# Divisor rows by fp32 matmul, a start by head, 16-row bit copies and a new filler rule in a fused attention and gated-convolution kernel

## The chip, the cores and the metric

The kernel runs on one core of one Trainium2 chip. The time is the device time of one execution in microseconds (us). Engines are named as in the profile: PE is TensorE's matmuls, PEld its weight loads, DVE is VectorE, ACT is ScalarE, POOL is GpSimd, SP is SyncE (it issues nearly all DMA transfers here, 269 of the 274 that the profile of before lists).

## The reference

Four batches, eight heads, 768 positions, head size 64. Attention is masked by hash buckets: each position gets six sign bits from a projection, and only keys with the same six bits count.

```python
q_bits = (einsum('bhsd,dk->bhsk', q, proj) > 0);  k_bits = ...
mask   = q_bucket[:, :, :, None] == k_bucket[:, :, None, :]
scores = where(mask, scale * (q @ k^T), -1e9)
attn   = exp(scores - max);  attn /= attn.sum(-1) + 1e-9
x      = (attn @ v) as (batch, 768, 512)
```

The result goes through a gated long convolution:

```python
x1, x2, x3 = split(x @ w_proj)                     # 3 x 512 columns
x2_conv    = irfft(rfft(x2) * rfft(filter_fft))    # along the 768 positions
out        = (x1 * x2_conv * x3) @ w_out
```

## The kernel before

The kernel works on "pairs": two heads of one batch, 16 pairs in all, four for each batch. For a pair, q and k are split into fp16 high and low parts (`hl`), transposed by DMA into `pr_q` and `pr_k` (channels on partitions), and the sign bits are written below the channels as extra rows of the contraction. A match adds a known constant to the score, so one biased exp does the masking.

The planner uses them for fillers: matmuls of a constant tile `warm`, whose result nobody reads, put into gaps that the planner expects on TensorE, meant to keep its clock up (its mean is 0.965 to 0.970 with 52 of them in e3 and 0.977 to 0.992 with 194 in e1, both below). This is the rule of before:

```python
WARM_COLS, WARM_UNTIL, WARM_FILL = 256, 115000.0, 0.7
if book.warm is not None and s < WARM_UNTIL and gap > 350.0 and before:
    room = w0 + WARM_FILL * gap         # 0.7 of a gap over 350 ns, until 115 us
    ...                                 # fillers of 256 columns while they fit
```

The bits are compared in one go into a tile `bt`, and four copies of 12 rows take them to their places:

```python
for i in range(4):
    nc.load(row[("q", "k")[i // 2]][HD : HD + NBIT, i % 2, :],
            bt[32 * i : 32 * i + NBIT, :], SMALL)      # NBIT = 12, SMALL = SyncE
```

After attention times v (`pv`, copied to `S` and summed to `T`), the row sums are turned by DMA (`lt`), inverted (`rl`), and spread over the 64 partitions of each head through a row in DRAM:

```python
nc.load(lt[:, par, :], S[r0 : r0 + 1, 0:SEQ], SMALL)                    # hop 1
...                                                                     # rl = 1 / lt
nc.load(rdr.rearrange("h (p c) -> p h c", p=P), rl, SMALL)              # hop 2, to DRAM
nc.load(R[HD*par : HD*par+HD, :], rdr[par:par+1, :].to_broadcast([HD, SEQ]), SMALL)  # hop 3
nc.vector.scalar_tensor_tensor(U, in0=T[:, 0:SEQ], scalar=vsd, op0=ALU.add, in1=R, op1=ALU.mult)
```

`U` is split again (`xh`, `xl`), and with the four pairs of a batch the projection can begin: its first matmuls are called `x2a`, its last ones `wout`. All instructions are recorded first; a planner with a cost for each then sets the order on each engine and writes it out. Every change of the program or of a cost therefore gives a new order of everything.

The softmax here doesn't subtract the row's maximum and nothing guards it: scores larger than these inputs give would overflow.

## Time and profile before

| | before |
|---|---|
| time, median | 463.37 us (the first three runs, 461.76 to 463.63; the result below has a fourth) |
| profiled span | 461.0 us |
| first score matmul | 14.7 us |
| first x2a (batch 0's projection) | 111.9 us |
| first wout | 190.8 us |
| span minus first wout | 270.2 us |

A chain here is the work followed back from the last instruction: at each step to what released it. The page of the kernel before, cut to the span, TensorE's busy tenths in 40 slices, its granted clock in tenths and the chain of work that ended last:

```profile
span 461.0 us, 7071 instructions
PE   7688987969899999999999999999999999999996
PEclk9789999879999999999999999999999999999999
...
PE 71%; DMA 12%; DVE 9%; ACT 3%; issue 3%; SPq 1%; DVEq 0%; ACTq 0%; POOLq 0%
PE x L232 24%; PE pv L232 10%; PE stp L232 9%; PE wout L232 9%; PE x2b L232 6%; PE x2a L232 6%; DMA pr_q<-hl 4%; PE zps L232 2%; DMA lt<-S 2%; ACT pt L232 2%; DMA w<-in_moe_w_proj_dram 2%; PE fdft L232 2%; DMA pr_k<-hl 1%; DMA R<-rdr 1%; DMA rdr<-rl 1%
```

The first ten slices (115 us) have holes and a clock that drops, to 7 or 8 tenths in four of them; later TensorE is full. The view by windows says the same; its columns are the stretch, its length, then the busy time of PE, PEld, DVE, ACT and POOL with instruction counts, the granted clock, the DMA share and GB/s:

```profile
80.00:100.00 20.00, 15.20 (x75) 6.43 (x75) 14.30 (x26) 8.62 (x13) 5.46 (x7) 0.80 0.89 195
180.00:200.00 20.00, 20.00 (x113) 10.85 (x112) 12.26 (x25) 12.39 (x17) 2.62 (x3) 1.00 0.77 183
200.00:460.00 260.00, 255.66 (x1519) 139.16 (x1517) 162.74 (x301) 125.47 (x182) 48.69 (x41) 1.00 0.25 65
```

From 180 us on TensorE is busy for 20.00 of 20 and 255.66 of 260 us, so there is little to win except by removing TensorE work. Before that, what TensorE waits for decides.

The next view is the timeline of TensorE in a stretch of before (start, length, engine, operation, count, and in brackets the idle time before and what ended it); `warm` marks fillers:

```profile
48.18 0.49 PE L232 MATMUL stp<-pr_q,pr_k 76*128 76x512 f16 x2
48.51 0.49 PE L229 MATMUL stp<-warm 128*128 128x256 f16 x3
49.06 0.48 PE L232 MATMUL stp<-pr_q,pr_k 76*128 76x512 f16 x2
49.39 0.49 PE L229 MATMUL stp<-warm 128*128 128x256 f16 x3
50.05 0.48 PE L232 MATMUL stp<-pr_q,pr_k 76*128 76x512 f16 x2 [0.17 <-ACT pt L232]
```

And ScalarE at the same time:

```profile
48.12 5.33 ACT L232 ACTIVATE pt<-stp,nmatch 128x768 f16<-128x768 f32 x6
```

Each pair of score matmuls is followed at once by its fillers, the fillers end before the exp of their tile begins, and ScalarE does six exps in 5.33 us, 0.89 us each, without a gap. Two score tiles are enough to keep it fed.

### The profile page before, as it was taken

The numbers are of one execution on the slowest core, as the hardware profiler recorded it, in microseconds if no ns is written. First come the engines' busy times: TensorE is split into PE (matmuls) and PEld (weight loads), VectorE is DVE, ScalarE is ACT, GpSimd is POOL, SyncE is SP. The second block draws the span as 40 slices with busy tenths as digits, with TensorE's granted clock in tenths as the row PEclk, the third lists the DMA queues.
The fourth block names the chain that finished last, engine by engine and source line by source line (L and its number), as shares of the span: only waits on it lengthen the run. The fifth ranks groups of instructions, "written<-read, shape, count | busy, mean of one in ns | idle before, by whom it ended". The sixth has DMA issues, their size and how long they took to land.

```text
span 461.0 us, 7071 instructions
## 1 busy us (share of the span) xinstructions
PE 431.6 (94%) x2590; PEld 233.4 (51%) x2590; DVE 305.9 (66%) x552; ACT 252.8 (55%) x348; POOL 112.2 (24%) x117
## 2 busy tenths in 40 slices
PE   7688987969899999999999999999999999999996
PEld 5244544425355456544455665544556664445652
DVE  4667687949593899734588879225677873279870
ACT  5679979358146752777565766665666632200102
POOL 4103297223031521212232211113242010122000
PEclk9789999879999999999999999999999999999999
DMA  9988679798845324765372323451010103100003
GB/s 273 201 213 207 159 213 251 165 202 216 201 110 148 86 58 76 183 162 155 79 135 71 75 71 74 141 131 48 3 40 2 34 4 107 66 0 1 0 2 137
DMA packets 101187, 51.88 MB, mean 113 GB/s; under 512 B 83520, under 2 KB 92816, under 8 KB 101152
## 3 DMA queue, kind: packets, MB, share of 16 engines
q1 hardware_dynamic: 99472, 51.00, 43.3%
q10 hardware_dynamic: 1552, 0.39, 0.4%
q8 instruction: 20, 0.33, 0.3%
q14 instruction: 15, 0.12, 0.1%
q0 software_dynamic: 128, 0.04, 0.0%
HBM read 32.02 MB, written 6.39 MB: 83 GB/s over the span
## 4 chain that ended last, share of the span: by engine, by line
PE 71%; DMA 12%; DVE 9%; ACT 3%; issue 3%; SPq 1%; DVEq 0%; ACTq 0%; POOLq 0%
PE x L232 24%; PE pv L232 10%; PE stp L232 9%; PE wout L232 9%; PE x2b L232 6%; PE x2a L232 6%; DMA pr_q<-hl 4%; PE zps L232 2%; DMA lt<-S 2%; ACT pt L232 2%; DMA w<-in_moe_w_proj_dram 2%; PE fdft L232 2%; DMA pr_k<-hl 1%; DMA R<-rdr 1%; DMA rdr<-rl 1%
## 5 line engine op out<-in xcount | busy, mean ns | idle before, releaser
L232 ACT ACTIVATE pt<-stp,nmatch 128x768 f16<-128x768 f32 x192 | 168.6, 899 | 65.1 <-PE stp L232 62.4
L232 PE MATMUL stp<-pr_q,pr_k 76*128 76x512 f16 (+1 forms) x384 | 96.3, 334 | 11.2 <-ACT pt L232 8.5
L232 PE MATMUL x<-xh,wph 128*128 128x384 f16 x256 | 83.4, 326 | 0.5 <-DVE bt L232 0.2
L232 PE MATMUL x<-xl,wph 128*128 128x384 f16 x256 | 83.4, 326 | 0.0
L232 PE MATMUL x<-xh,wpl 128*128 128x384 f16 x256 | 83.4, 326 | 0.0
L232 PE MATMUL pv<-pt,vt 128*128 128x257 f16 (+1 forms) x384 | 76.4, 333 | 1.4 <-DVE bt L232 1.4
L232 PEld LDWEIGHTS <-wph 128*128 128x128 f16 x512 | 49.7, 97 | 34.6 <-issue 2.2
L232 DVE SCALAR_TENSOR_TENSOR T<-S,cst_sb,pv 64x512 f32<-64x512 f32 x64 | 38.3, 608 | 36.8 <-ACT S L232 35.9
L232 PEld LDWEIGHTS <-pr_k 76*128 76x128 f16 x384 | 36.9, 99 | 49.8 <-issue 22.8
L232 POOL TENSOR_TENSOR xl<-R,xh 128x768 f16<-128x768 f32 x16 | 26.3, 1641 | 133.1 <-DVE xh L232 112.4
L232 PEld LDWEIGHTS <-vt 128*128 128x128 f16 x384 | 37.8, 99 | 29.8 <-issue 5.9
L232 ACT COPY S<-pv 64x512 f32<-64x512 f32 (+1 forms) x48 | 22.8, 476 | 43.1 <-PE pv L232 39.1
L232 PEld LDWEIGHTS <-wpl 128*128 128x128 f16 x256 | 25.0, 97 | 16.1
L232 POOL TENSOR_TENSOR vt<-nat_v,vt 128x768 f16<-128x768 f32 x16 | 26.2, 1641 | 17.9 <-ACT vt L232 17.0
L232 PEld LDWEIGHTS <-xh 128*128 128x128 f16 x192 | 18.7, 97 | 20.7 <-issue 0.3
L232 DVE TENSOR_SCALAR bt<-zps,cst_sb 128x384 f16<-128x384 f32 x30 | 17.5, 610 | 16.2 <-PE zps L232 15.7
L232 ACT ACTIVATE osb<-wout 128x512 f32<-128x512 f32 x24 | 14.3, 596 | 24.7 <-PE wout L232 24.6
L232 POOL CAST vt<-nat_v 128x768 f16<-128x768 f32 x11 | 9.0, 823 | 74.1 <-PE pv L232 74.1
L232 DVE SCALAR_TENSOR_TENSOR R<-T,vsd,R 128x768 f32<-128x768 f32 x16 | 16.2, 1012 | 14.6 <-DMA R<-rdr 14.6
L232 DVE SCALAR_TENSOR_TENSOR hl<-nat_k,hl 128x768 f16<-128x768 f32 x16 | 16.3, 1016 | 12.2 <-ACT hl L232 12.1
L232 DVE TENSOR_TENSOR fu<-x2b,x2s 128x512 f32<-128x512 f32 x12 | 8.3, 688 | 23.6 <-PE x2b L232 23.6
L232 ACT ACTIVATE hl<-nat_k 128x768 f16<-128x768 f32 x16 | 13.5, 844 | 14.7 <-DMA pr_k<-hl 9.1
(339 smaller groups left out, 673.5 us busy)
## 6 DMA issues: line engine op xcount, KB each, us to landing
nat_k<-in_k_dram SPq DMA_DIRECT2D x16, 384.0 KB
nat_v<-in_v_dram SPq DMA_DIRECT2D x16, 384.0 KB
R<-rdr SPq DMA_DIRECT2D x32, 192.0 KB
out_dram<-osb SPq DMA_DIRECT2D x24, 256.0 KB
nat_q<-in_q_dram SPq DMA_DIRECT2D x15, 384.0 KB
w<-in_moe_w_proj_dram SPq DMA_DIRECT2D x12, 256.0 KB
w<-in_moe_filter_fft_dram SPq DMA_DIRECT2D x6, 256.0 KB
w<-in_moe_w_out_dram SPq DMA_DIRECT2D x4, 256.0 KB
```

Source lines behind the costliest of these rows:

```text
L232: o["done"] = getattr(getattr(nc, o["lane"]), o["method"])(*[sub(x) for x in o["args"]], **{n: sub(x) for n, x in o["kw"].items()})
```

## The change

Its intent was to start earlier and to shorten the way from `T` to `U`, and so to bring the first x2a forward. It has six parts: (1) for pairs 0 to 3 and 15, the rows of `rl` are spread by an fp32 matmul with a selector `sel` instead of the DRAM row; (2) the first pair is prepared head by head, and the loads behind it are held until its data are in work; (3) bit rows in copies of 16 instead of 12; (4) the queues of the bit copies and of the weight loads get constants of their own, which name SyncE, as before, so this part changes nothing; (5) new costs in the planner, among them a model of shared DMA time; (6) a new rule for fillers.

The core of the diff, with cuts marked (the remark behind `R_PE` is this document's):

```diff
+ROWS = 16
...
-            if book.warm is not None and s < WARM_UNTIL and gap > 350.0 and before:
+            if book.warm is not None and gap > 40.0 and before:
                 w0 = free[e]
-                room = w0 + WARM_FILL * gap
-                while True:
-                    ... # pieces of 256 columns
+                while w0 < s:
+                    cold = active.get(int(w0 // 3413) - 1, 0.0) < 1640.0
+                    if not cold and gap < WARM_GAP:
+                        break
+                    room = free[e] + WARM_FILL[0 if cold else 1] * gap - w0
+                    c = [n for n in WARM_COLS if n / (1.2 if cold else 2.4) <= room]
...
-WARM_COLS, WARM_UNTIL, WARM_FILL = 256, 115000.0, 0.7
+WARM_COLS, WARM_GAP, WARM_FILL = (256, 128, 64), 350.0, (1.0, 0.9)
...
-                row[("q", "k")[i // 2]][HD : HD + NBIT, i % 2, :], bt[32 * i : 32 * i + NBIT, :], SMALL
+                row[("q", "k")[i // 2]][HD : HD + ROWS, i % 2, :], bt[32 * i : 32 * i + ROWS, :], BITQ
...
+        if g in R_PE:                      # R_PE = (0, 1, 2, 3, 15)
+            row = U[0:2, :]
+            for par in range(2):
+                nc.load(row[par : par + 1, :], rl[:, par, :], SMALL)
+            for hf in range(2):
+                rp = psW.tile([P, HALF], FP32, tag="w", name="rp")
+                nc.tensor.matmul(rp, sel, row[:, cs])
+                nc.vector.scalar_tensor_tensor(U[:, cs], in0=T[:, cs], scalar=vsd,
+                    op0=ALU.add, in1=rp, op1=ALU.mult)
+        else:
+            ...                            # the DRAM row, as before
...
-        load_qk(0, "p", "s")
-        hilo(0)
-        turn_pe(0)
-        zbits(0, True)
+        for par in range(2):
+            first_loads(par)
+        first_turn(0)
+        load_qk(1, None, None, True)
+        first_turn(1)
...                                        # new planner costs, cut
```

## The prediction

> **What bounds the kernel now.** The windows view splits the 461.0 us span in two. From 180 us on TensorE is nearly always busy. Before that the chain of waits runs through "DMA pr_q<-hl", "lt<-S", "rdr<-rl", ACT and DVE. Counting TensorE's order at its warm pace (512 columns 0.216 us, 384 columns 0.162, sixteen zps 0.76) gives about 391 us of work, 57 us of it ahead of the first x2a, which starts at 111.95 us. So about 41 us are lost there (half-clock stretches, waits, 126 fillers of 13 us) and about 15 us later. Only the first loss is worth attacking.
>
> Why: (a) The first score matmul starts at 14.74 us, after `ident` (5.5 us on the GpSimd queue), two-head transposes and bits. (b) SyncE is nearly full: from 28 to 112 us its issues last 74 of 84 us (timeline): transposes 1.4 to 2.4 us, 12-row bit copies 0.8 us each, four per pair, the 128-row `lt` 0.55. (c) From the end of T to U take 18, 23, 26 and 26 us for pairs 0 to 3: three DMA hops, one through DRAM, then DVE's order. Pair 3's U (108.95 us) gates x2a.
>
> **What the change does.**
> - Pairs 0 to 3 and 15: the DRAM row and two 192 KB broadcasts become two row copies and two fp32 matmuls: one hop and 0.39 MB less per pair. [...]
> - 16-row bit copies: [...]I expect 0.55 us, 1 us of SyncE per pair.
> - First pair by head: first scores at about 11 us; zps of pair 1 at 19 us, from 22.7.
> - New planner costs: the built order moves x2a from after 144 score matmuls to after 132; fillers 126 to 224, now also beyond 115 us, where a planned gap stands around ida (about 3 us of fillers).
>
> **Sum.** Up to pair 3's U, SyncE's issues would end near 70 us, ACT (60 exps of 0.9 us, hl, vt) near 77, DMA (share 0.8 to 0.9, less broadcasts) near 80. Waits among them add some 10: first x2a at about 91 us. After it stand 340 us of TensorE work (4.7 us done ahead before now come later, and one rp pair) and about 17 us of loss: span 448; the timed runs lie 2.4 us above the traced span.
>
> Predicted 450 us (3% faster), 440 to 459 eight times in ten; faster by over 2% 0.70, within 2% 0.26, slower 0.04.
>
> **What would show it.** First score near 11 us; `pr<-bt` issues near 0.55 us; T to U under 15 us for pairs 0 to 3; first x2a at 86 to 96 us; ACT busier from 20 to 90 us; rp about 0.65 us; after x2a the same saturation.
>
> **What would make it wrong.** DMA engines, not SyncE, may hold the transposes (the share reaches 1.14 at 90 to 100 us): x2a then stays beyond 100 us. The gap around ida may exceed its fillers, or weights come late. DVE's order may hold U though the row is ready. If the new order fits the chip better than I allow, x2a comes before 85 us.

## More of the kernel before

Runs of one kernel still differ by 1 to 7 us, so a single trace shows a mechanism well and a difference of 2 us badly.

One score tile is 128 keys by 768 queries. It lies in a PSUM tile of 1024 fp32 columns, of which there are two:

```python
stp = psS.tile([P, 1024], FP32, tag="s", name="stp")        # two buffers
for lo_c, hi_c in ((0, 512), (512, SEQ)): ...               # SEQ is 768; two matmuls, cut
    nc.tensor.matmul(stp[:, lo_c:hi_c], kp[kr, ts(jt, P)], qp[kr, lo_c:hi_c])
nc.scalar.activation(pt[:, 0:SEQ], stp[:, 0:SEQ], AF.Exp, bias=nmatch, scale=LSCALE)
```

The last 256 columns of the tile hold no scores.

## The result

| | before | after |
|---|---|---|
| time, median | 462.56 us (four runs, 461.74 to 463.63) | 478.46 us (four runs, 477.80 to 480.20) |
| ratio, 95% interval | | 1.0348, 1.0309 to 1.0387: slower |
| profiled span | 461.0 us | 476.0 us |
| first score matmul | 14.7 us | 11.0 us |
| first x2a | 111.9 us | 119.2 us |
| first wout | 190.8 us | 204.0 us |
| span minus first wout | 270.2 us | 272.0 us |

Ratios, here and below, are ratios of fast runs, with a 95% interval; they are not quite the ratio of the medians that are quoted.

The change makes the kernel 3.5% slower. Of the 15.0 us that the span is longer, 13.2 us are there at the first wout; what comes after takes the same time within 2 us. The page of the kernel after, the lines that answer to those of before:

```profile
span 476.0 us, 7319 instructions
PE   8797969969999999999999999999999999999996
PEclk9797897989999999999999999999999999999999
...
PE 79%; DVE 14%; ACT 4%; issue 2%; DVEq 0%; ACTq 0%
PE x L245 22%; PE pv L245 12%; PE stp L245 12%; PE wout L245 9%; PE x2a L245 7%; PE x2b L245 7%; PE stp L198 4%; ACT pt L245 4%; PE zps L245 2%; DVE hl L245 2%; DVE cv L245 2%; PE fdft L245 1%; DVE uv L245 1%; PE rp L245 1%; PE idrq L245 1%
```

Fillers (`stp L198`) and exps (`ACT pt`) are now in the chain that ended last, with 4% each; in before the fillers were not in it and the exps had 2%. The waits through DMA that the change aimed at (`DMA lt<-S`, `rdr<-rl`, `R<-rdr`) are no longer among the fifteen largest; DMA, with 12% of the chain before, is not in it at all, and VectorE has 14% in place of 9%. So something of what was intended happened, and another thing came beside it. TensorE's windows of after, to be read against those of before:

```profile
80.00:100.00 20.00, 16.70 (x99) 8.86 (x99) 13.96 (x18) 13.39 (x18) 13.81 (x12) 0.91 0.74 163
180.00:200.00 20.00, 19.37 (x134) 11.47 (x133) 19.62 (x43) 6.75 (x11) 1.65 (x1) 1.00 0.68 159
200.00:460.00 260.00, 259.09 (x1537) 141.04 (x1536) 163.88 (x321) 129.66 (x187) 32.51 (x29) 1.00 0.24 63
```

TensorE is busier from 80 to 100 us than before (16.70 against 15.20 us) and yet later with its work: the fillers in this stretch take 3.14 us, in before 0.93 us. Where the time goes is seen in the timeline of TensorE in a stretch of after with the same work as the one shown of before:

```profile
37.56 0.24 PE L198 MATMUL stp<-warm 128*128 128x128 f16 x2 [0.99 <-ACT pt L245]
37.65 0.49 PE L245 MATMUL stp<-pr_q,pr_k 80*128 80x512 f16 x2
37.98 0.49 PE L198 MATMUL stp<-warm 128*128 128x256 f16 x3
39.52 0.32 PE L198 MATMUL stp<-warm 128*128 128x128 f16 x2 [1.05 <-ACT pt L245]
39.65 0.83 PE L245 MATMUL stp<-pr_q,pr_k 80*128 80x512 f16 x2
40.27 0.85 PE L198 MATMUL stp<-warm 128*128 128x256 f16 x3
42.16 0.32 PE L198 MATMUL stp<-warm 128*128 128x128 f16 x2 [1.05 <-ACT pt L245]
42.30 0.83 PE L245 MATMUL stp<-pr_q,pr_k 80*128 80x512 f16 x2
```

and of ScalarE:

```profile
36.61 0.90 ACT L245 ACTIVATE pt<-stp,nmatch 128x768 f16<-128x768 f32 x1 [0.17 <-PE stp L198]
38.56 0.90 ACT L245 ACTIVATE pt<-stp,nmatch 128x768 f16<-128x768 f32 x1 [1.05 <-PE stp L198]
41.21 0.90 ACT L245 ACTIVATE pt<-stp,nmatch 128x768 f16<-128x768 f32 x1 [1.75 <-PE stp L198]
```

Read them as one story. At 36.61 us an exp begins. TensorE's next instruction is a filler of 128 columns into the same tile as that exp reads. It waits until the exp is over (idle 0.99 us, ended by ScalarE) and starts at 37.56 us. The next scores go to the other tile, which is free, but they stand behind the filler in TensorE's order and start at 37.65 us; three more fillers into their tile follow and end at 38.47 us. Only then does the next exp begin, at 38.56 us. The exps now come 1.95 us and 2.65 us apart instead of 0.89 us: the two tiles no longer overlap. The second distance is longer also because the clock fell: from 39.5 to 44 us it was granted at 0.50, and two score matmuls take 0.83 us instead of 0.49.

The filler writes columns 768 to 895 of the tile and the exp reads columns 0 to 767, so the two touch no common element; what they share is the tile. Yet the trace of after has the waits, 15 of them, 15.4 us in all. They are in the built program (15 of the 224 fillers carry one), so they are set before it runs; by which part of the software, and by what rule, no run here tells.

How much it adds up to is shown by the waits of the whole run (in total us, times, longest). First after:

```profile
PE stp L198 <- ACT pt L245: 15.4, 15, 1.1
ACT pt L245 <- PE stp L198: 12.8, 18, 1.7
```

Before has no line of the first kind, and of the second only the first line here; the other shows that its score matmuls waited for exps too, which those of after do not:

```profile
ACT pt L232 <- PE stp L229: 0.3, 2, 0.2
PE stp L232 <- ACT pt L232: 8.5, 16, 4.0
```

Fifteen waits of 1.0 us each: the size of the whole loss. That is a coincidence until experiments confirm it, the more so as part of the 15.4 us stands in place of the 8.5 us.

### The profile page after: what moved, and what is told of

Its sections match the earlier page's. It is cut to its first block, busy times and chain, and to the rows that moved or that the text cites. A ratio compares the mean times of both kernels' runs of the same rounds, so it can differ in the third digit from the quotient of the medians.

```text
span 476.0 us, 7319 instructions
## 1 busy us (share of the span) xinstructions
PE 448.0 (94%) x2708; PEld 244.6 (51%) x2708; DVE 311.8 (66%) x580; ACT 253.8 (53%) x350; POOL 97.6 (20%) x102
## 4 chain that ended last, share of the span: by engine, by line
PE 79%; DVE 14%; ACT 4%; issue 2%; DVEq 0%; ACTq 0%
PE x L245 22%; PE pv L245 12%; PE stp L245 12%; PE wout L245 9%; PE x2a L245 7%; PE x2b L245 7%; PE stp L198 4%; ACT pt L245 4%; PE zps L245 2%; DVE hl L245 2%; DVE cv L245 2%; PE fdft L245 1%; DVE uv L245 1%; PE rp L245 1%; PE idrq L245 1%
## 5 line engine op out<-in xcount | busy, mean ns | idle before, releaser
L245 ACT ACTIVATE pt<-stp,nmatch 128x768 f16<-128x768 f32 x192 | 170.9, 900 | 96.5 <-PE stp L245 79.0
L245 PE MATMUL stp<-pr_q,pr_k 80*128 80x512 f16 (+1 forms) x384 | 97.1, 337 | 0.7 <-DVE pr_q L245 0.3
L245 PE MATMUL pv<-pt,vt 128*128 128x257 f16 (+1 forms) x384 | 77.8, 336 | 1.6 <-DVE hB L245 1.2
L245 POOL TENSOR_TENSOR xl<-R,xh 128x768 f16<-128x768 f32 x16 | 28.3, 1771 | 163.7 <-DVE xh L245 154.6
L245 PEld LDWEIGHTS <-pr_k 80*128 80x128 f16 x384 | 36.4, 100 | 44.1 <-issue 18.4
L198 PE MATMUL stp<-warm 128*128 128x256 f16 (+2 forms) x223 | 34.7, 293 | 15.4 <-ACT pt L245 15.4
L245 POOL TENSOR_TENSOR vt<-nat_v,vt 128x768 f16<-128x768 f32 x16 | 27.7, 1734 | 43.9 <-ACT vt L245 20.9
L198 PEld LDWEIGHTS <-warm 128*128 128x128 f16 x223 | 23.9, 108 | 20.4 <-issue 13.4
L245 POOL CAST vt<-nat_v 128x768 f16<-128x768 f32 x8 | 6.7, 843 | 71.8 <-PE pv L245 71.8
L245 DVE SCALAR_TENSOR_TENSOR hl<-nat_k,hl 128x768 f16<-128x768 f32 (+1 forms) x17 | 15.4, 903 | 8.8 <-ACT hl L245 7.5
```

The lines of the kernel that those rows point to most:

```text
L198: nc.tensor.matmul(bank[:, SEQ : SEQ + n], sub(w), sub(z[:, 0:n]))
L245: o["done"] = getattr(getattr(nc, o["lane"]), o["method"])(*[sub(x) for x in o["args"]], **{n: sub(x) for n, x in o["kw"].items()})
```

## The experiments

All medians are of four runs (of j2, five), each beside runs of before on the same chip. "First x2a" and "first wout" are from the profiled run. Five chips were used (for e1 to e4; f1 to f4; f5 and the h; the i; the j), so between these groups the ratios are to be compared and not the medians. Unless it is said that the order is kept, the planner made a new one for the kernel.

| kernel | median us | ratio to before (95%) | span | first x2a | first wout |
|---|---|---|---|---|---|
| after | 478.46 | 1.0348 (1.0309 to 1.0387) | 476.0 | 119.2 | 204.0 |
| e1 after, late fillers dropped | 465.19 | 1.0035 (0.9977 to 1.0094) | 463.2 | 102.7 | 189.7 |
| e2 after, 0.7 of the gaps | 461.59 | 0.9959 (0.9916 to 1.0003) | 459.7 | 99.2 | 188.1 |
| e3 after, no fillers once exps run | 463.90 | 1.0019 (0.9973 to 1.0066) | 463.6 | 104.9 | 191.8 |
| e4 before, new filler rule | 478.20 | 1.0329 (1.0293 to 1.0365) | 476.3 | 126.2 | 204.0 |
| f1 before, 16 rows | 455.46 | 0.9864 (0.9810 to 0.9918) | 457.3 | 108.4 | 187.3 |
| f2 before, spreading by matmul | 467.44 | 1.0106 (1.0051 to 1.0160) | 465.4 | 105.0 | 194.7 |
| f4 before, new planner costs | 466.67 | 1.0090 (1.0041 to 1.0139) | 464.4 | 109.9 | 192.4 |
| i3 before, new start and loads | 464.80 | 1.0048 (1.0002 to 1.0095) | 460.6 | 110.5 | 189.7 |
| f3 after's program, old planner and fillers | 457.40 | 0.9884 (0.9822 to 0.9945) | 458.2 | 106.3 | 187.3 |
| i4 f3 without the spreading | 459.86 | 0.9938 (0.9913 to 0.9962) | 458.3 | 111.9 | 187.1 |
| i1 f3, spreading for pair 3 alone | 458.40 | 0.9903 (0.9873 to 0.9934) | 457.0 | 112.5 | 186.4 |
| f5 e1 without the spreading | 460.23 | 0.9942 (0.9895 to 0.9988) | 457.9 | 106.0 | 186.6 |
| i5 e2, spreading for pair 3 alone | 467.55 | 1.0098 (1.0041 to 1.0156) | 466.4 | 109.2 | 194.1 |
| h3 f2 with its fp32 matmuls twice | 470.31 | 1.0158 (1.0095 to 1.0221) | 467.8 | 106.5 | 193.7 |
| j1 e1, four VectorE instructions twice | 470.20 | 1.0166 (1.0095 to 1.0237) | 469.9 | 110.7 | 196.9 |
| j2 e1, the same four off VectorE | 461.33 | 0.9986 (0.9918 to 1.0054) | 465.9 | 107.1 | 193.8 |
| h2 before, 16 rows, spreading for pair 3 | 455.34 | 0.9828 (0.9777 to 0.9878) | 453.8 | 104.6 | 183.3 |

One more kernel (h1, f3 without the spreading and without its late fillers) came out at 459.60 us, 0.9928 (0.9879 to 0.9978), the same as i4. All but j2 gave correct results.

### Is it the fillers?

The theory: fillers that stand behind the exp of their own tile wait for it and block the scores. The rivals: the spreading by matmul, the new planner costs or the new start cause the loss.

First, e1: the order of after is kept to the last instruction (in the traces of both, the 2484 matmuls that are no fillers stand in the same order), and only those fillers are left out that stand behind the exp of their tile. These are 30 of 224.

```diff
                 if k < 0:
+                    if read.get(bank):          # the tile was last touched by its reader
+                        continue
                     self.fill(nc, real[bank], -k, sub)
...
+                for t in self.ops[k]["touch"]:
+                    read[t] = o["lane"] != "tensor"
```

> The changed kernel in the same planned order, without the 30 fillers that are written after the exp of their own score tile (15 of the 224 wait for ScalarE in the program; before, none did). Theory ([...]a late filler waits for exp and holds the next score matmul: 15 waits of about 1 us and the same again in the exp after it): 455 to 465 us, idle before fillers near 0 (15.4 us in the changed kernel), pairs 1 to 3 of batch 0 take 13 to 15 us of scores each instead of 17 to 21. Rival (the new planner costs or the fp32 spreading made the order slow, and the fillers only stand in gaps that are there anyway): 474 to 480 us.

Measured: 465.19 us, 13.3 us less than after (median against median), and the first x2a 16.6 us earlier. The waits of fillers for ScalarE are gone from the view; of the other kind this is left:

```profile
ACT pt L250 <- PE stp L198: 1.9, 7, 0.8
```

So the late fillers make the loss of after. Their waits are the greater part of what e1 takes away, but not all: the page of after has 34.7 us of fillers and that of e1 27.4 us, so the 30 also took some 7 us of TensorE time. The two were not tested apart. A lower clock can hardly be the cause: e4, the next kernel, is as slow at a mean granted clock of 0.986, against 0.978 in the profiled run of before.

Second, e4, the opposite: before's program, with nothing new but the filler rule and the order that the planner then makes (356 fillers, 14 of which carry a wait for ScalarE in the built program).

> The kernel before with only the new filler rule (356 fillers, 14 wait for ScalarE). Theory: slower than before by 8 to 20 us (470 to 483 us), with idle of about 1 us before fillers put down to exp, and TensorE's late stage also lengthened by fillers beyond 115 us. Rival: within 2 % of before (454 to 472 us).

Measured: 478.20 us, 15.5 us over before of the same rounds (462.66 us), with the same two lines in its waits:

```profile
PE stp L229 <- ACT pt L232: 14.3, 14, 1.1
ACT pt L232 <- PE stp L229: 11.8, 18, 1.9
```

So the filler rule alone, with the order that comes of it, makes the whole loss in the old program, and taking away 30 of 224 fillers undoes it in the new one. Neither the spreading nor the start nor the costs are needed for it. That the late fillers do it in e4 too is likely by these lines, but e4 was not run without them.

Third, e2 keeps the new rule but lets it fill only 0.7 of a gap: 116 fillers, one with a wait.

```diff
-WARM_COLS, WARM_GAP, WARM_FILL = (256, 128, 64), 350.0, (1.0, 0.9)
+WARM_COLS, WARM_GAP, WARM_FILL = (256, 128, 64), 350.0, (0.7, 0.7)
```

> One constant of the changed kernel back: fillers fill 0.7 of a planned gap, not 1.0 and 0.9 (116 fillers, 1 waits for ScalarE; the planned order may differ a little). Theory: 453 to 465 us, as the dropped fillers. Rival (order, not fillers): 474 us or more.

Measured: 461.59 us, with a single wait of a filler for ScalarE of 1.0 us in the trace. Which filler comes late is settled in the plan: instructions are written out in the order of their planned starts, so a filler that is planned past the start of its tile's exp is written behind it. With a margin at the end of the gap this befalls only one of them. The order of e2 was made anew, so it is a weaker test than e1.

Fourth, e3 asks, with the order of after kept, what the fillers are worth at all: none after the first exp, 52 are left from the start.

```diff
                 if k < 0:
+                    if scored:                  # the first exp has been written out
+                        continue
```

> The changed kernel in the same order, all fillers after the first exp dropped (52 are left). It asks what the fillers are worth for the clock. Theory: the waits go too, but the mean granted clock falls below 0.95 and more matmuls before 120 us run at half pace: 458 to 472 us, above the run that drops only the late ones. Rival: 474 us or more.

Measured: 463.90 us, not to be told from e1 (465.19) or before. The clock was expected to fall below 0.95 and the time to rise above e1; neither came. The mean granted clock of the four runs is 0.965 to 0.970, against 0.977 to 0.992 in e1, and the time does not show it. TensorE's waits for exps are not gone either, they now stand before scores:

```profile
PE stp L249 <- ACT pt L249: 11.6, 18, 2.0
```

Here 11.6 us of such waits cost nothing that the time shows, and 15.4 us before late fillers went with a loss of 13 us. So it is not their sum alone that counts. The timeline above suggests what does: a waiting filler also holds scores for a tile that is free. The mean granted clock is lower with the fewer fillers of e3 than in e1, by the figures above, but in this kernel what a higher clock gains in time is too small to be seen, and the loss that came with the late fillers is large (13.3 us).

### What each of the other parts is worth alone

f1 is before with 16 rows in the bit copies and nothing else (`NBIT` becomes `ROWS = 16` in the two slices of each copy and in the contraction).

> The kernel before with 16-row bit copies alone. Theory (SyncE's issue time is one of the things that hold the first 110 us, and 12 rows cost 0.8 us per issue): issues at about 0.55 us as in the changed kernel, 4 us less issue time from 28 to 112 us, total 458 to 462 us. Rival (SyncE only follows the data, its time is not on the chain): issues shorter, total within 0.3 % of before.

Measured: 455.46 us, 1.4% faster, more than was expected; the profiled run, with 459.11 us, is the slowest of the four. The view of tile `bt` gives the issue times on SyncE as minimum, median and maximum in ns; first before, then f1:

```profile
L232 SPq DMA_DIRECT2D pr_q<-bt x30: 717/780/918, 24.9 to 333.2; - x30
L232 SPq DMA_DIRECT2D pr_k<-bt x30: 714/720/1072, 26.8 to 334.8; - x30
```

```profile
L233 SPq DMA_DIRECT2D pr_q<-bt x30: 517/550/622, 25.1 to 329.4; - x30
L233 SPq DMA_DIRECT2D pr_k<-bt x30: 511/540/1074, 26.5 to 330.6; - x30
```

The copies of 16 rows take less time to issue here than those of 12: 0.54 to 0.55 instead of 0.72 to 0.78 us (medians). Why they do is not shown. That the gain in time comes from the shorter issues is not shown apart: the planner's order moved a little as well.

f2 is before with the spreading by matmul for pairs 0 to 3 and 15 and nothing else (the block `if g in R_PE` of the diff above, the load of `sel`, and in the planner the change's cost of an fp32 matmul).

> The kernel before with the divisor rows of pairs 0 to 3 and 15 spread by matmul alone (old planner, old fillers, 82 of them). Theory (pair 3's U gates the first x2a): T to U falls from 18 to 26 us to about 14 us, first x2a 5 to 10 us earlier, total 452 to 459 us. Rival (what follows x2a has a bound of its own, DVE and batch 1's attention, that absorbs it): x2a earlier, total 459 to 464 us.

Measured: 467.44 us, 1.1% slower, although the first x2a comes at 105.0 instead of 111.9 us. From the end of `T` to `U` it takes 14.8, 15.5, 13.8 and 11.9 us for pairs 0 to 3, where before took 18, 23, 26 and 26. The mechanism works, and the time gets worse, which neither side of the expectation had. One reason may be in this line pair of f2's timeline:

```profile
65.86 2.92 PE L232 MATMUL rp<-R,sel 2*128 2x384 f32 x4
...
70.48 0.90 ACT L232 ACTIVATE pt<-stp,nmatch 128x768 f16<-128x768 f32 x1 [5.18 <-PE stp L232]
```

TensorE, at a granted clock of 0.50 from 65 to 69 us, does two fp32 matmuls for 2.92 us in front of scores and `pv`, and ScalarE sits idle 5.18 us. Each matmul shows as two records (20 for ten in after). In the whole of f2 its ten matmuls take 9.1 us by the groups of instructions, in after 7.8 us:

```profile
L245 PE MATMUL rp<-R,sel 2*128 2x384 f32 x20 | 7.8, 507 | 0.0
```

The other may be where the gain was sought; neither was tested apart. In f2 only 124 score matmuls stand ahead of the first x2a, in before 144. Some of what x2a gains by coming early is work that now stands behind it, and the first wout comes 3.9 us later than before.

f4 is before's program with the new planner costs and the old filler rule, i3 is before with the new start and the held loads alone.

> The old body under the new planner costs with the old filler rule (110 fillers, 2 wait). If the new costs alone help: 452 to 459 us. If they are neutral: 459 to 465 us. If they are part of the loss: above 466 us.

> The kernel before with the by-head start and the held first loads alone (12 rows, DRAM rows for all pairs, old planner and filler rule; 129 fillers, 1 waits). If the 3 us earlier first score is kept to the end: 458 to 461 us. If it is lost before the saturated stage: 461 to 466 us.

Measured: f4 466.67 us, 0.9% slower; i3 464.80 us, 0.5% slower, though in the latter the first score stands at 11.3 us, 3.5 us earlier than before. That advance is lost by the first wout (189.7 against 190.8 us). Why the new costs give a worse order was not looked into further.

f3 is the sum of the good and the doubtful: the program of after, with the planner costs and the filler rule of before.

> The changed body (by-head start, held loads, 16 rows, spreading by matmul) under the old planner with its costs and filler rule. If the body is worth what I predicted: 448 to 456 us. If the body is worth little and only the fillers hurt: 458 to 464 us, as with the fillers thinned. If the body itself hurts under the old costs: above 466 us.

Measured: 457.40 us, 1.2% faster than before. Under the old planner the change's program is a small gain; it was the planner half of the diff that lost it.

### Does the spreading help in some order?

f5 is e1 with `R_PE = ()`, so with the DRAM row for all pairs.

> The changed kernel with late fillers dropped and without the spreading by matmul. Theory: below the same with it (465 us), 456 to 462 us. Rival (the new planner's order needs the shorter chain): 465 us or more.

Measured: 460.23 us against 465.19 us of e1. Without the spreading the kernel seems faster, though its first x2a is 3.4 us later: the same sign as f2. The intervals of the two ratios just overlap (up to 0.9988, and from 0.9977).

i4 and h1 do the same to f3, i4 with all fillers and h1 without the two late ones.

> The changed body under the old planner without spreading by matmul, with all its fillers (134, 2 wait for ScalarE). If the dropped fillers cost clock there: 454 to 458 us. If they did not matter: 458 to 462 us, as with them dropped.

> The changed body under the old planner (by-head start, held loads, 16 rows), without the spreading by matmul: all pairs take the DRAM row; late fillers dropped. Theory (the fp32 matmuls cost more than the hop they save, because TensorE's order puts them ahead of the next scores): faster than the same body with them, 449 to 455 us. Rival (their cost in the kernel before alone came from that order, not from them): 456 to 460 us.

Measured: 459.86 and 459.60 us against 457.40 us of f3. Here the spreading seems to help a little, but the intervals overlap (0.9913 to 0.9962 for i4, 0.9822 to 0.9945 for f3).

h3 is f2 with each of the ten fp32 matmuls issued twice, to measure their price; the order was planned anew.

```diff
                 nc.tensor.matmul(rp, sel, row[:, cs])
+                nc.tensor.matmul(rp, sel, row[:, cs])
```

> The kernel before with spreading by matmul, each fp32 matmul issued twice (10 more, about 0.74 us each). Theory (they stand on TensorE's line in front of scores, so their time is paid): 5 to 10 us above the single ones, 471 to 477 us. Rival (they lie in idle time, as I predicted, and something else of that version costs): within 2 us of the single ones, 465 to 469 us.

Measured: 470.31 us, 2.9 us over f2 in the median. Ten more matmuls of 0.91 us, f2's mean, would be 9.1 us if each delayed the end; about a third shows. The intervals of f2 and h3 overlap, so this is a size and not a proof. Nor is it paid where it was looked for: in the traces h3 has its first wout 1.0 us earlier than f2, and the longer time comes after it.

i1 keeps only pair 3's spreading in f3 (pair 3 being the last one that batch 0's projection needs), and i5 does so in e2.

> The changed body under the old planner with spreading for pair 3 alone (126 fillers, 2 wait). If its gains add to those of 16 rows with pair 3 in the old body (455 us): 450 to 455 us. If the start adds nothing: 455 to 460 us.

> The changed kernel with fillers at 0.7 of a gap and spreading for pair 3 alone (206 fillers, 2 wait). If the four other spreadings cost 4 us there: 455 to 459 us, beating the kernel before. If they cost nothing: 460 to 464 us.

Measured: i1 458.40 us (0.9903), between f3 and i4 and with an interval that overlaps both. i5 467.55 us, 1.4% worse than e2 and outside what was expected; but its planned gaps differ, and it has 206 fillers, two of them with a wait, against 116 and one. So the sign of the spreading depends on the order that the planner makes around it, and it stays open which property of the order decides.

### What else held back the first x2a

The prediction put the first x2a at 91 us. Without the late fillers it stands at 102.7 us, so 11.6 us of that error are not the fillers' doing. The window of e1 from 80 to 100 us points at VectorE (third pair of numbers, 19.60 of 20 us), with the DMA share at 0.51:

```profile
80.00:100.00 20.00, 17.12 (x89) 7.61 (x87) 19.60 (x27) 11.51 (x16) 11.96 (x10) 0.91 0.51 140
```

The first x2a itself waits for VectorE:

```profile
102.65 0.38 PE L250 MATMUL x2a<-wph,xh 128*128 128x512 f16 x1 [0.40 <-DVE T L250]
```

Two kernels test it with all orders kept. j1 issues the four instructions for the low halves of pairs 6 and 7 twice. j2 takes them off VectorE and puts a plain copy on GpSimd in their place, with a wrong result.

```diff
+                if k in low:                 # j2; j1 issues the instruction once more instead
+                    o["done"] = nc.gpsimd.tensor_copy(sub(o["args"][0]), sub(o["kw"]["in0"]))
+                    continue
```

> The kernel after without its late fillers, in which four VectorE instructions (the low halves of q and k of pairs 6 and 7, 0.95 us each, three of them between 86 and 101 us) are issued twice; all other orders stay as they are. Theory: from 75 us to the first x2a (102.65 us) VectorE's order is the limit (19.60 of 20 us busy from 80 to 100 us), so the first x2a comes 2.9 to 3.8 us later, at 105.5 to 106.5 us. Rival: SyncE's issues or the DMA (share 0.51 there) gate it, and VectorE only looks full: the first x2a moves by less than 1 us. The time may move less than x2a does, because the first wout is what counts: 465 to 469 us by the theory, 464 to 466 by the rival.

> The kernel after without its late fillers, in which the same four instructions are taken from VectorE and stand on GpSimd instead, as plain copies of the same shape (wrong result on purpose: the low halves hold something else). Theory of VectorE's order: the first x2a comes 2.5 to 4.6 us earlier than 102.65, at 98 to 100 us. Rival (SyncE or DMA): it stays within 1 us of 102.65. The time follows x2a only as far as the first wout (189.7 us) does: 461 to 465 us.

Measured: j1 has `U` of pair 1 at about the same time as e1 (63.5 and 63.8 us), before its edit acts, and then the first x2a 8.1 us later than e1; the four added instructions took 1.91, 1.79, 2.28 and 0.96 us, together 6.9 us. Only 2.9 to 3.8 us had been expected. Its ratio is 1.0166 against 1.0035 of e1, with intervals that just do not meet. So work added to VectorE there delays the first x2a. That it is paid one for one is not shown: the delay is larger than the work, the profiled run is the slowest of the four (471.71 us), and VectorE is busy for 18.17 us from 80 to 100 us in it, less than in e1. j2 gave no such clear answer. Its profile fell on the slowest of its five runs (467.73 us); in it, `U` of pair 1 is already 3.9 us later than in e1, before the edit acts, and from there to the first x2a it takes 39.4 us, where e1 took 38.8: nothing gained. Its other four runs lie between 460.97 and 462.10 us, which would be some 4 us less than e1, but the intervals of j2 and e1 overlap widely, and 3.9 us is also how far two traces can differ where nothing was changed. VectorE is thus shown as something the stretch cannot bear more of. That it is the only limit is not shown, and the trace of j2 speaks against it: `T` of pair 4 waits there 1.28 and 1.74 us for ScalarE's copies.

### A kernel that beats both

h2 is before with 16 rows and with the spreading for pair 3 alone.

> 16-row bits and the spreading for pair 3 alone, whose U gates the first x2a (2 fp32 matmuls). If the gate is worth something and the cost is per matmul: 452 to 456 us, at or below 16 rows alone. If an earlier x2a gains nothing because the work that moves behind it comes later: 455 to 459 us.

Measured: 455.34 us, ratio 0.9828 to before (0.9777 to 0.9878), and 23 us less than after. f1, with the 16 rows alone, has 455.46 us (0.9864, 0.9810 to 0.9918). The two cannot be told apart, so what is sure of this gain is what f1 has alone: the 16 rows, with the order planned for them.

## Why the prediction was wrong

The prediction said 450 us, at least 440 and at most 459; the kernel took 478.46 us. Point by point:

- **First score near 11 us: right.** It starts at 11.0 us.
- **Issues of the 16-row copies near 0.55 us: right.** Their medians are 0.54 and 0.56 us in after, against 0.72 and 0.78 us for 12 rows in before. The 0.55 us was the author's estimate. Alone they are worth 1.4%.
- **rp about 0.65 us: low.** The figure was the author's estimate; before has no fp32 matmul to read it from. Measured: 7.8 us for ten in after, 0.78 us each, and in f2 1.46 us each where the clock was granted at 0.50. An fp16 matmul of the same 384 columns takes 0.162 us in before, from one start to the next at a granted clock of 1.00.
- **"After it stand 340 us of TensorE work ... and about 17 us of loss": right.** From the first x2a to the end after takes 476.0 − 119.2 = 356.8 us, against 357 us as predicted. That it fits so closely is luck in part: the same order without its late fillers takes 360.5 us (e1), and before takes 349.1 us.
- **T to U under 15 us: wrong in after, nearly right without its late fillers.** After: about 17, 20, 17 and 10.5 us; e1: 14.0, 15.1, 13.8 and 10.7 us.
- **ACT busier from 20 to 90 us: wrong.** It is busy for 46.1 of these 70 us, before for 54.3.
- **First x2a at 86 to 96 us: wrong,** and this is the whole error: 119.2 us, 28 us after the 91 us that the sum used.

The step that failed first is how the prediction counted the fillers. It wrote "fillers 126 to 224, now also beyond 115 us, where a planned gap stands around ida (about 3 us of fillers)": the fillers were taken to lie in gaps, and its sum has no term for what they cost. The runs showed a cost in that place: a filler that the planner put behind the exp of its tile waits for that exp, about 1.03 us each, with the scores of the other tile behind it. Fifteen such waits make 15.4 us; dropping the late fillers takes 13.3 us off the time and 16.6 us off the first x2a, and the new rule alone adds 15.5 us to before. The lengths of fillers that are not late hardly count: e1 keeps 194, which its page has busy for 27.4 us, and is no slower than e3 with 52. How the loss divides between the waits of the 30 late ones and their own 7 us is not shown.

The second step that failed is the sum for the first x2a: "SyncE's issues would end near 70 us, ACT ... near 77, DMA ... near 80 ... Waits among them add some 10". It has no term for VectorE, which is busy 19.60 of 20 us from 80 to 100 us once the fillers are out of the way. The prediction did name this under what would make it wrong ("DVE's order may hold U though the row is ready"), without giving it a number. j1 shows that more work for VectorE delays the first x2a; how much of the 11.6 us is VectorE's own is not settled.

The third is the milestone. The prediction took the first x2a as what decides. In before, after and all kernels of the table, the time from the first wout to the end is 270 to 274.1 us, so the time follows the first wout. An earlier x2a is partly paid back before it: e1 has its first x2a 9.3 us earlier than before, its first wout only 1.1 us earlier, and its span is 2.2 us longer.

Without the filler rule, then, the rest of the change is worth nothing measurable (e1: 1.0035, 0.9977 to 1.0094). It consists of a gain from the 16 rows (0.9864 alone) and of small losses by the new costs (1.0090), the spreading (1.0106) and the new start (1.0048). The product of these four is 1.011, which is more than e1 shows; every part re-plans the whole order, so the parts do not simply multiply.

## What to carry to other kernels

An instruction inserted to keep an engine warm is not free because a gap was planned for it (here 15 of 224 waited, 15.4 us in all): look at what it writes, who else uses that tile, and what stands behind it in the order, and leave a margin between the planned gap and the fill. When a change brings its own scheduler tuning, test that apart from the program, since here one line of constants (0.7 of a gap in place of 1.0 and 0.9) outweighed all the work on the program. Choose as milestone the last point after which the engine is saturated, not the first sign of progress before it.
